# Pausing the weight steps in one-slot jobs and spacing the weights' sum from its use, in a Fourier transform with a mixture-of-experts layer

## The chip, the cores and the metric

The kernel runs on one core of a Trainium2 chip. The metric is device time in microseconds (us): the time from the start to the end of one execution on that core. Engines are named as in the profile: PE (TensorE, matmuls; PEld its weight loads), ACT (ScalarE), DVE (VectorE), POOL (GpSimd) and SP (SyncE, which here only issues DMAs).

## The reference

```python
X = np.fft.fft(x, axis=1)              # x: 8 x 1856 x 256
X = np.fft.fft(X, axis=2)
x = X.real.astype(np.float32).reshape(14848, 256)
...
g_idx = np.argmax(x @ w_group, axis=1)           # one of 4 groups for each token
e_idx = np.argmax(xg @ w_expert[g], axis=1)      # one of 4 experts of that group
h = np.maximum(xg[mask_e] @ w1[g, e], 0.0)       # 256 -> 1024
ye = h @ w2[g, e]                                # 1024 -> 256
out[tok_idx] = (g_w * e_w)[:, None] * ye         # two softmax weights
```

Each of 14848 tokens goes through the one expert (of 16) that its two argmaxes choose.

## The kernel before, in words

**Phase 1** computes the transform and the routing, and writes a row for each token to a DRAM table. **Phase 2** (`phase2`, L1335) runs the experts; the change lies there alone.

*Slots and jobs.* Tokens of one expert are gathered in slots of 128 rows. A job is one unit of weights and one to four slots. There are 44 jobs. Jobs 0 to 5 serve experts 0 to 2. Then each expert from 3 on has a four-slot job and a three-slot job, and all but the last are followed by a one-slot job for overflow rows, whose expert is known only at run time: job 8 (the ninth) is the first of these, then 11, 14 and so on to 41. So from job 6 on the work goes in groups of three jobs: four slots, three slots, one slot.

*One job.* Float32 values are split into a high and a low float16 half, and each product is made of three float16 matmuls (high x high, high x low, low x high). `layer1` (L1286) has eight groups; each makes one tile `ph` (128 x 512, 384 or 128 columns for four, three or one slots) with six matmuls, three for each half of the 256 inputs; the third and the sixth use the low half of the weights. ACT (L1299) and DVE (L1300) then take `ph` out into `hT`. `layer2` (L1305) makes one tile `py` for each slot with 24 matmuls of 256 columns; ACT takes it out into `y` (L1317) and POOL scatters the rows. PSUM has four banks for `ph` and two for `py`. The second layer of a job runs in the iteration of the next job, after that job's first layer: `pend` holds it.

*Weights.* The float32 weights of a unit (128 x 4096, 2 MB) land in `wst` by four DMAs of 512 KB that SP issues (`load_weights`, L1180). `split_steps` (L1193) is a generator that makes the float16 halves `whl` from them, one step for each call: four squares on ACT with a sum each (`junk`, `wacc`), two empty steps (`lag`), two small matmuls `pn` that sum over partitions (L1207) and one yield, then on DVE the scale (`e_ei`, two `e_v`, `winv`), and then four times a high half on ACT and a low half on DVE, 1024 columns at a time. Columns 0 to 2047 are the first layer's weights (parts 0 and 1), the rest the second layer's. The call after the last step takes the result and lets SP issue the loads of the next unit.

*Who hands out the steps.* `tick(g, t)` (L1457) is called after each group of a first layer with t = T1 x slots = 320 x slots, and after each slot of a second layer with t = T2 = 2570. It adds t to a balance and calls `weights()` (L1406) once for every 800 in it (`RATE2`). `weights()` runs one step of the first unit in `todo`, unless that unit's `whl` tile still belongs to a unit whose last job is not done: `free(todo[0]) > state["done"]`, where `done` becomes n - 1 at the end of iteration n (L1488). Then it returns False and the balance is set to 0. Units of long experts rotate over three `whl` tiles; the one-slot units have one of their own. `tick` also advances `g`, which casts (`xh`, L1258, L1260) and transposes (L1266, a DMA transpose from SP) the gathered rows of the next job.

```python
def tick(g, t):
    state["t"] += t
    rate = RATE if state["tail"] else RATE2
    while state["t"] >= rate:
        state["t"] = state["t"] - rate if weights() else 0
    tail()
    if not state["tail"]:
        next(g, None)
```

*The order on each engine.* The squares, halves and scales are issued through wrappers that keep them in program order (`self.V`, `self.A`); the rest of phase 2 is placed by the framework's scheduler, engine by engine. On each engine the order is fixed in the program, and each instruction waits for its operands there.

Of the kernel before, what the change touches and what calls it, by code (L numbers as in the profile page):

```python
# [46 lines left out]
LASTZ = 7  # L47
LATER = 3
OVER_AT = 4

RATE, RATE2, T1, T2 = 1000, 800, 320, 2570

# [199 lines left out]
def pow2s(V, pool, sumsq, n, tag, outs):  # L252

    ei = pool.tile([P, n], I32, name=f"{tag}_ei", tag=f"{tag}_ei")
    V.tensor_scalar(out=ei, in0=sumsq.bitcast(I32), scalar1=24, scalar2=None,
                    op0=ALU.logical_shift_right)
    vs = []
    for k, (m, a) in enumerate(outs):
        v = pool.tile([P, n], F32, name=f"{tag}_v{k}", tag=f"{tag}_v{k}")
        V.tensor_scalar(out=v.bitcast(I32), in0=ei, scalar1=m * E23, scalar2=a * E23,  # L260
                        op0=ALU.mult, op1=ALU.add)
        vs.append(v)
    return ei, vs


def top(ap):

    return ap.bitcast(mybir.dt.bfloat16).rearrange("p (n t) -> p n t", t=2)[:, :, 1]
# [34 lines left out]
class K:  # L303
# [886 lines left out]
                self.tc.keep_in_program_order(ins)  # L1190
        return st

    def split_steps(self, wp, st, V, A, M, pn, lag=0):  # L1193


        sm = self.sm
        acc = sm.tile([P, 2, 2], F32, name="wacc")
        junk = self.cp.tile([P, 4 * 257], mybir.dt.bfloat16, name="junk", tag="junk")
        for h in range(4):
            A.activation(junk[:, 0:1024], st[:, h * 1024:(h + 1) * 1024], AF.Square,  # L1200
                         accum_out=acc[:, h // 2, h % 2:h % 2 + 1])
            yield
        for _ in range(lag):
            yield
        acc = top(acc.rearrange("p a h -> p (a h)")).rearrange("p (a h) -> p a h", h=2)
        for h in range(2):
            M.matmul(pn, lhsT=self.one_b, rhs=acc[:, :, h], start=h == 0, stop=h == 1)  # L1207
        yield
        _, (sw, isw) = pow2s(V, sm, pn, 2, "e", [(-1, 198), (1, 56)])
        inv = sm.tile([P, 1], F32, name="winv", bufs=4)  # L1210
        V.tensor_tensor(out=inv, in0=isw[:, 0:1], in1=isw[:, 1:2], op=ALU.mult)
        yield
        w = wp.tile([P, 2, 4096], F16, name="whl")
        for i in range(4096 // WPART):
            s = slice(i * WPART, (i + 1) * WPART)
            h = i * WPART // 2048
            A.activation(w[:, 0, s], st[:, s], AF.Copy, scale=sw[:, h:h + 1])
            yield
            V.scalar_tensor_tensor(out=w[:, 1, s], in0=st[:, s], scalar=sw[:, h:h + 1],
                                   in1=w[:, 0, s], op0=ALU.mult, op1=ALU.subtract)  # L1220
            yield
        return w, inv
# [112 lines left out]
    def phase2(self, wp):  # L1335
        tc, nc = self.tc, self.nc
        wpa = self.wpa
        with tc.tile_pool(name="h", bufs=2, reuse_waits="tile") as hp, \
# [26 lines left out]
            def pools(u):  # L1365
                kind, e = units[u]
                if kind == "o":
                    return "wo", "wo"
                return "w", ("wa", "w2", "wx")[e % 3]
# [9 lines left out]
            st, ready, infos, xs, want = {}, {0: self.w0}, {}, {}, []  # L1379
            self.scratch = wpx.tile([P, 2, 4096], F16, name="whl").rearrange("p h n -> p (h n)")  # L1380
            state = dict(split=None, done=-1, t=0, tail=self.last_rows(), job=0)
            begun = lambda u: u < len(first) or state["job"] >= LATER

            def tail():
                if state["tail"]:
                    try:
                        next(state["tail"])
                    except StopIteration:
                        state["tail"] = None
                        pool["wo"] = later.enter_context(  # L1390
                            tc.tile_pool(name="wo", bufs=1, side="right", reuse_waits="tile"))
                    serve()
# [7 lines left out]
            def loads():  # L1400
                for u in todo:
                    if u not in st and all(pools(v)[0] != pools(u)[0] for v in st) and pools(u)[0] in pool \
                            and (units[u][0] == "s" or "o" in infos) and begun(u):
                        load(u)

            def weights():  # L1406

                if state["split"] is None:
                    if not todo or free(todo[0]) > state["done"] or (units[todo[0]][0] == "o" and "o" not in infos) \
                            or not begun(todo[0]):  # L1410
                        return False
                    loads()
                    pn = self.misc[:, 490 + 2 * todo[0]:492 + 2 * todo[0]] if state["tail"] else self.ps.tile([P, 2], F32, name="pn", tag="misc")
                    state["split"] = self.split_steps(pool[pools(todo[0])[1]], st[todo[0]],
                                                      self.V, self.A, nc.tensor, pn, 2)
                try:
                    next(state["split"])
                except StopIteration as e:
                    u = todo.pop(0)
                    ready[u], state["split"] = e.value, None  # L1420
                    del st[u]
                    loads()
                return True
# [25 lines left out]
            def prep(n):  # L1449
                if n < len(jobs):  # L1450
                    while n in want:
                        tail()
                    xs[n] = self.x0[n] if n < len(self.x0) else \
                        (yield from self.turn_steps(qp, *xs[n], *((self.V, self.A) if jobs[n][1] == "e" else
                                                                  (nc.vector, nc.scalar)), nc.sync))

            def tick(g, t):  # L1457
                state["t"] += t
                rate = RATE if state["tail"] else RATE2
                while state["t"] >= rate:  # L1460
# [4 lines that stand above are left out]
# [7 lines left out]
            for n, (u, kind, slots) in enumerate(jobs):  # L1472
                while u not in ready:
                    assert weights()
                w, inv = ready[u]
                state["job"] = n
                if n == OVER_AT:
                    infos["o"] = self.overflow_info(pool["wo"])
                g = prep(n + 1)
                xT, wt = xs.pop(n)  # L1480
                cw, toks = self.slot_weights(qp, wt, inv)
                fetch(n + 2)
                for _ in range(2 * len(jobs[2][2]) if n == 1 else 0):
                    next(g, None)
                hT = finish(self.layer1(hp, w, xT, len(slots)), lambda: tick(g, T1 * len(slots)))
                if pend:
                    finish(self.layer2(*pend), lambda: tick(g, T2))
                    state["done"] = n - 1  # L1488
                for _ in g:
                    pass  # L1490
                pend = (qp, w, hT, cw, toks)
# [79 lines left out]
```

## Time and profile before

| what | value |
|---|---|
| three runs | 891.83, 895.41, 895.62 us, median 895.41 |
| the profiled execution | 892.05 us, its span 890.2 us |
| PE busy in the span | 823.2 us (92%) |
| DVE, ACT, POOL busy | 546.6, 577.0, 313.5 us |
| first one-slot job that the change reaches | about 402 us into the span |

The page has one line for the busy time of each engine, then a line per engine with 40 slices of the span. The timeline merges instructions of the same kind that follow each other: start, length, engine, line, operation, out<-in, shape, count, and in brackets the idle time of the engine before them with what ended it. Times in it are from the span's start. Ends of matmuls are modelled.

### The profile page before, as it was taken

Reading aid. Unit: us, or ns where it says so; the run is one execution under the profiler, and the core shown is the slowest. Engines: PE = TensorE matmul, PEld = TensorE weight load, DVE = VectorE, ACT = ScalarE, POOL = GpSimd, SP = SyncE. Lnnn points to the kernel's source line nnn. Section 1 sums busy time; section 2 is a strip of 40 time slices with the busy share of each in tenths; the row PEclk is TensorE's granted clock in tenths of the full one; section 3 lists DMA queues with packets and bytes.
Section 4 is the critical chain, followed back from the end, with each engine's and each line's share of the span. In section 5 each row is a group of like instructions: output and inputs, shape, how many; then the busy total and the mean of one; then the engine's idle time right before and its main releaser. Section 6 shows DMA issues by size and latency. Waiting matters only on the chain.

```text
span 890.2 us, 17777 instructions
## 1 busy us (share of the span) xinstructions
PE 823.2 (92%) x6491; PEld 587.2 (66%) x6491; DVE 546.6 (61%) x1381; ACT 577.0 (65%) x1190; POOL 313.5 (35%) x326
## 2 busy tenths in 40 slices
PE   2799999889697999999999999999999999999996
PEld 0367666556455767776767676767676768686865
DVE  6479998579574656464747474747474756564440
ACT  2477676576633877586858585858686777775541
POOL 1032211412674524434343434344343435240303
PEclk9999999899999999999999999999999999999999
DMA  9677863364667355555646454646555746443201
GB/s 351 176 226 201 243 210 121 137 210 138 186 180 197 111 189 181 158 155 166 173 156 178 149 166 155 173 160 172 161 176 152 196 147 206 127 137 66 55 10 41
DMA packets 105515, 144.53 MB, mean 162 GB/s; under 512 B 75194, under 2 KB 77638, under 8 KB 103888
## 3 DMA queue, kind: packets, MB, share of 16 engines
q1 hardware_dynamic: 91360, 106.15, 39.4%
q0 software_dynamic: 13632, 36.99, 14.5%
q8 instruction: 52, 0.85, 0.4%
q10 hardware_dynamic: 432, 0.22, 0.1%
q14 instruction: 39, 0.32, 0.1%
HBM read 97.41 MB, written 31.72 MB: 145 GB/s over the span
## 4 chain that ended last, share of the span: by engine, by line
PE 58%; DVE 11%; issue 8%; ACT 5%; DMA 5%; POOL 2%; another core or an unknown queue 2%; SPq 1%; POOLq 0%; DVEq 0%; ACTq 0%
PE ph L1296 29%; PE py L1312 24%; DMA xT<-xh 3%; PE pu L281 2%; ACT whl L281 2%; POOL out L940 2%; PE pr L281 1%; DVE whl L281 1%; DMA wst<-w 1%; DVE xq L281 1%; ACT junk L281 1%; SPq L1266 1%; DVE ghl L281 1%; DVE xT L281 1%
## 5 line engine op out<-in xcount | busy, mean ns | idle before, releaser
L1312 PE MATMUL py<-whl,hT 128*128 128x256 f16 x2976 | 357.4, 273 | 13.6 <-ACT y L1317 9.8
L1296 PE MATMUL ph<-xT,whl 128*128 128x512 f16 (+2 forms) x2112 | 358.4, 318 | 10.6 <-DMA xT<-xh 4.8
L1312 PEld LDWEIGHTS <-hT 128*128 128x128 f16 x2976 | 289.2, 98 | 71.4 <-issue 15.2
L1300 DVE SCALAR_TENSOR_TENSOR hT<-ph,hT 128x512 f16<-128x512 f32 (+2 forms) x352 | 179.7, 529 | 194.1 <-ACT hT L1299 126.6
L1296 PEld LDWEIGHTS <-whl 128*128 128x128 f16 x2112 | 182.5, 98 | 134.1 <-issue 16.6
L940 POOL DMA_INDIRECT out<-y,tok x124 | 147.3, 1188 | 332.2 <-ACT y L1317 266.2
L1299 ACT ACTIVATE hT<-ph 128x512 f16<-128x512 f32 (+2 forms) x352 | 157.2, 473 | 116.0 <-PE ph L1296 68.1
L281 DVE SCALAR_TENSOR_TENSOR whl<-wst,e_v,whl 128x1024 f16<-128x1024 f32 x112 | 138.0, 1279 | 20.1 <-ACT whl L281 18.0
L1238 POOL DMA_INDIRECT xg<-XS,ii_s x100 | 105.5, 1055 | 86.7 <-ACT xh L1258 35.7
L281 ACT ACTIVATE whl<-wst,e_v 128x1024 f16<-128x1024 f32 x112 | 121.0, 1138 | 15.2 <-DVE e_v L281 11.4
L281 ACT ACTIVATE junk<-wst 128x1024 bf16<-128x1024 f32 x112 | 119.2, 1064 | 6.0 <-DMA wst<-w 5.1
L1317 ACT ACTIVATE y<-py,cws 128x256 f32<-128x256 f32 x124 | 57.2, 471 | 52.0 <-PE py L1312 41.2
L281 PE MATMUL pu<-CS,ghl 128*128 128x464 f16 (+3 forms) x384 | 83.8, 370 | 3.5 <-ACT ghl L281 3.5
L1260 DVE TENSOR_TENSOR xh<-xg,xh 128x256 f16<-128x256 f32 x112 | 46.3, 418 | 48.7 <-ACT xh L1258 35.7
L1258 ACT CAST xh<-xg 128x256 f16<-128x256 f32 x112 | 42.4, 402 | 38.6 <-DMA xT<-xh 34.7
L281 PEld LDWEIGHTS <-ghl 128*128 128x128 f16 (+1 forms) x384 | 44.5, 120 | 33.2 <-issue 3.6
L281 PEld LDWEIGHTS <-U 128*128 128x128 f16 x672 | 44.9, 100 | 19.2 <-issue 7.0
L281 PE MATMUL pr<-c,U 128*128 128x256 f16 x336 | 49.9, 286 | 4.9 <-DMA U<-un 2.5
L281 ACT CAST U<-pu 128x464 f16<-128x464 f32 (+3 forms) x64 | 32.8, 548 | 20.0 <-PE pu L281 19.0
L281 POOL DMA_DIRECT2D xq<-xq x12 | 11.0, 1072 | 88.5 <-ACT xT L281 27.1
L281 DVE TENSOR_TENSOR xq<-xq 128x514 f32<-128x514 f32 x40 | 25.4, 688 | 6.4 <-DMA xq<-xq 6.2
L281 ACT ACTIVATION_READ_ACCUMULATOR junk<-wst 128x1 f32 x112 | 23.2, 207 | 0.0
(184 smaller groups left out, 461.1 us busy)
## 6 DMA issues: line engine op xcount, KB each, us to landing
wst<-w SPq DMA_DIRECT2D x108, 512.0 KB
xq<-xq SPq DMA_DIRECT2D x8, 1028.0 KB
xq<-xq POOLq DMA_DIRECT2D x12, 514.0 KB
XS<-whl SPq DMA_DIRECT2D x6, 910.0 KB
CS<-cs SPq DMA_DIRECT2D x8, 464.5 KB
XS<-row SPq DMA_DIRECT2D x3, 1040.0 KB
XS<-row SPq DMA_DIRECT2D x3, 910.0 KB
XS<-xq SPq DMA_DIRECT2D x3, 910.0 KB
```

Source lines behind the costliest of these rows:

```text
L281: return self.tc.keep_in_program_order(f(*args, **kw))
L940: ins = self.nc.gpsimd.indirect_dma_start(out=out, out_offset=bass.IndirectOffsetOnAxis(ap=ap, axis=0), in_=in_, in_offset=None, bounds_ch ...
L1238: ins = self.nc.gpsimd.indirect_dma_start(out=xg[:, :].bitcast(I32), out_offset=None, in_=self.XS[:, :], in_offset=bass.IndirectOffsetOnAx ...
L1258: A.copy(xh[:, 0], xg[:, 0:D])
L1260: lo = V.tensor_tensor(out=xh[:, 1], in0=xg[:, 0:D], in1=xh[:, 0], op=ALU.subtract)
L1266: Q.dma_start(out=xT[:, :, j * P:(j + 1) * P], in_=xh, transpose=True)
L1296: nc.tensor.matmul(ph[:, 0:n * P], lhsT=w[:, wl, o:o + P], rhs=xT[:, xl * 2 + c, :], start=i == 0, stop=i == 5)
L1299: nc.scalar.activation(hT[:, f, 0], ph[:, 0:n * P], AF.Relu)
L1300: nc.vector.scalar_tensor_tensor(out=hT[:, f, 1], in0=ph[:, 0:n * P], scalar=0.0, in1=hT[:, f, 0], op0=ALU.max, op1=ALU.subtract)
L1312: nc.tensor.matmul(py, lhsT=hT[:, f, hl, j * P:(j + 1) * P], rhs=w[:, wl, 2048 + f * D:2048 + (f + 1) * D], start=i == 0, stop=i == 23)
L1317: nc.scalar.activation(y, py, AF.Copy, scale=cw)
```

## The change

From the ninth job on (`STEADY = 8`) `tick` hands out no step during the first layer of a job with one slot (there t is T1), and leaves the balance as it is; it still advances `g`. And for units whose split begins from the ninth job on, two more empty steps lie between the `pn` matmuls and the scale on DVE (`late` = 2).

```diff
+STEADY = 8
...
-    def split_steps(self, wp, st, V, A, M, pn, lag=0):
+    def split_steps(self, wp, st, V, A, M, pn, lag=0, late=0):
...
         for h in range(2):
             M.matmul(pn, lhsT=self.one_b, rhs=acc[:, :, h], start=h == 0, stop=h == 1)
-        yield
+        for _ in range(1 + late):
+            yield
         _, (sw, isw) = pow2s(V, sm, pn, 2, "e", [(-1, 198), (1, 56)])
...
                     state["split"] = self.split_steps(pool[pools(todo[0])[1]], st[todo[0]],
-                                                      self.V, self.A, nc.tensor, pn, 2)
+                                                      self.V, self.A, nc.tensor, pn, 2, 2 if state["job"] >= STEADY else 0)
...
             def tick(g, t):
+                if t == T1 and state["job"] >= STEADY:
+                    return next(g, None)
                 state["t"] += t
```

What that does to the order is seen at three places; the same repeats in each group of three jobs. Line numbers in the changed kernel are one or two higher.

ACT around a one-slot job's first layer, before: the last three evictions of the three-slot first layer, y of the second slot, the four high halves of the one-slot unit in a block, then casts and the y of the third and fourth slot.

```order
L1299 ACTIVATE hT<-ph 128x384
L281 ACTIVATE junk,wacc<-wst 128x1024
L1299 ACTIVATE hT<-ph 128x384 x3
L1317 ACTIVATE y<-py,cws 128x256
L281 ACTIVATE whl<-wst,e_v_5041 128x1024 x4
L1258 CAST xh<-xg 128x256
L1317 ACTIVATE y<-py,cws 128x256
L1258 CAST xh<-xg 128x256 x2
L1317 ACTIVATE y<-py,cws 128x256
L1299 ACTIVATE hT<-ph 128x128 x4
```

The same place now:

```order
L282 ACTIVATE junk,wacc<-wst 128x1024 x2
L1301 ACTIVATE hT<-ph 128x384
L1319 ACTIVATE y<-py,cws 128x256
L1301 ACTIVATE hT<-ph 128x384
L282 ACTIVATE whl<-wst,e_v_5101 128x1024 x2
L1319 ACTIVATE y<-py,cws 128x256
L282 ACTIVATE whl<-wst,e_v_5101 128x1024
L1260 CAST xh<-xg 128x256 x3
L1319 ACTIVATE y<-py,cws 128x256
L282 ACTIVATE whl<-wst,e_v_5101 128x1024
L1301 ACTIVATE hT<-ph 128x128 x4
```

The y of the third slot stands behind two high halves where it stood behind four, and the y of the fourth slot behind three high halves and three casts, with the fourth high half after it.

PE at the end of the first four groups of a one-slot first layer, before (`ph` and `py` with their numbers): the last matmul of each group, which reads the low half of part 1, stands directly ahead of the three-slot job's second layer.

```order
L1296 MATMUL ph_5207<-xT_4961,whl_5077 128x128
L1296 LDWEIGHTS whl_5077
L1296 MATMUL ph_5220<-xT_4961,whl_5077 128x128
L1296 LDWEIGHTS whl_5077
L1296 MATMUL ph_5232<-xT_4961,whl_5077 128x128
L1296 LDWEIGHTS whl_5077
L1296 MATMUL ph_5243<-xT_4961,whl_5077 128x128
L1296 LDWEIGHTS whl_5077
L1296 MATMUL ph_5243<-xT_4961,whl_5077 128x128
L1312 LDWEIGHTS hT_4945
L1312 MATMUL py_5301<-whl_4194,hT_4945 128x256
```

The same place now:

```order
L1314 LDWEIGHTS hT_4943
L1314 MATMUL py_5301<-whl_4194,hT_4943 128x256
L1298 LDWEIGHTS whl_5107
L1298 MATMUL ph_5207<-xT_4955,whl_5107 128x128
L1298 LDWEIGHTS whl_5107
L1298 MATMUL ph_5220<-xT_4955,whl_5107 128x128
L1298 LDWEIGHTS whl_5107
L1298 MATMUL ph_5232<-xT_4955,whl_5107 128x128
L1298 LDWEIGHTS whl_5107
L1298 MATMUL ph_5243<-xT_4955,whl_5107 128x128
```

Ahead of these four matmuls now stand 16 to 19 of the 24 matmuls of the first `py`. The second `pn` matmul moved too: 43 `py` matmuls stood between it and the one-slot first layer, and 31 stand there now.

DVE where a long unit's low halves end and the three-slot first layer begins, before: all four low halves are done ahead of that layer's first eviction.

```order
L281 SCALAR_TENSOR_TENSOR whl<-wst,e_v_4848,whl 128x1024
L1300 SCALAR_TENSOR_TENSOR hT<-ph,hT 128x512
L281 SCALAR_TENSOR_TENSOR whl<-wst,e_v_4848,whl 128x1024 x3
L281 TENSOR_SCALAR cws<-wt,winv 128x3
L281 CAST tok<-wt 128x3
L1260 TENSOR_TENSOR xh<-xg,xh 128x256
L1261 SCALAR_TENSOR_TENSOR wt<-ge_s,xg 128x2
L1300 SCALAR_TENSOR_TENSOR hT<-ph,hT 128x384
```

The same place now:

```order
L1302 SCALAR_TENSOR_TENSOR hT<-ph,hT 128x512
L282 SCALAR_TENSOR_TENSOR whl<-wst,e_v_4871,whl 128x1024 x3
L282 TENSOR_SCALAR cws<-wt,winv 128x3
L282 CAST tok<-wt 128x3
L1262 TENSOR_TENSOR xh<-xg,xh 128x256
L1263 SCALAR_TENSOR_TENSOR wt<-ge_s,xg 128x2
L1302 SCALAR_TENSOR_TENSOR hT<-ph,hT 128x384
L1262 TENSOR_TENSOR xh<-xg,xh 128x256
L1263 SCALAR_TENSOR_TENSOR wt<-ge_s,xg 128x2
L1302 SCALAR_TENSOR_TENSOR hT<-ph,hT 128x384
L282 SCALAR_TENSOR_TENSOR whl<-wst,e_v_4871,whl 128x1024
```

The fourth low half now stands behind two evictions of the three-slot first layer; SP's loads of the next long unit, which write the same `wst`, wait for it. SP's own order is the same in both.

## Rows read from the trace of the kernel before

**Rows 1.** The page: the span and the busy time of each engine.
```profile
span 890.2 us, 17777 instructions
...
PE 823.2 (92%) x6491; PEld 587.2 (66%) x6491; DVE 546.6 (61%) x1381; ACT 577.0 (65%) x1190; POOL 313.5 (35%) x326
```
**Rows 2.** Stretches of 40 us: length, PE, PEld, DVE, ACT, POOL busy; clock; DMA.
```profile
480.00:520.00 40.00, 38.68 (x313) 28.24 (x312) 23.32 (x54) 28.06 (x58) 15.01 (x14) 1.00 0.55 159
...
sum 400.00, PE 389.96 PEld 287.29 DVE 236.84 ACT 285.86 POOL 162.42; mean PE 39.00 PEld 28.73 DVE 23.68 ACT 28.59 POOL 16.24
```
**Rows 3.** Waits of PE, 395 to 800 us: us in total, times, longest.
```profile
PE py L1312 <- ACT y L1317: 7.4, 10, 0.8
PE ph L1296 <- DVE whl L281: 2.0, 7, 0.4
```
**Rows 4.** PE's timeline at the first and the last of nine one-slot jobs.
```profile
403.77 0.93 PE L1312 MATMUL py<-whl,hT 128*128 128x256 f16 x7 [0.81 <-ACT y L1317]
...
750.62 1.58 PE L1312 MATMUL py<-whl,hT 128*128 128x256 f16 x13 [0.81 <-ACT y L1317]
```
**Rows 5.** Timeline of all engines, 784 to 795 us: the tenth one-slot job.
```profile
787.18 0.15 DVE L281 TENSOR_SCALAR e_ei<-pn 128x2 int32<-128x2 int32 x1
...
791.18 1.50 PE L1296 MATMUL ph<-xT,whl 128*128 128x128 f16 x24
...
792.55 2.67 PE L1312 MATMUL py<-whl,hT 128*128 128x256 f16 x23
```
**Rows 6.** PE's timeline, 470 to 496 us: the one-slot job at 487.88.
```profile
473.47 1.14 PE L1296 MATMUL ph<-xT,whl 128*128 128x384 f16 x6
...
481.71 0.65 PE L1296 MATMUL ph<-xT,whl 128*128 128x384 f16 x3
...
482.85 0.17 PE L1207 MATMUL pn<-wacc,one_b 128*128 128x2 bf16 x1
...
485.26 2.78 PE L1312 MATMUL py<-whl,hT 128*128 128x256 f16 x24 [0.15 <-ACT y L1317]
487.88 1.22 PE L1296 MATMUL ph<-xT,whl 128*128 128x128 f16 x19
489.46 0.45 PE L1296 MATMUL ph<-xT,whl 128*128 128x128 f16 x5 [0.36 <-DVE whl L281]
490.73 5.07 PE L1312 MATMUL py<-whl,hT 128*128 128x256 f16 x45 [0.81 <-ACT y L1317]
```
**Rows 7.** ACT's timeline in the same place.
```profile
484.36 0.49 ACT L1299 ACTIVATE hT<-ph 128x384 f16<-128x384 f32 x1 [2.23 <-PE pn L1207]
...
485.74 4.27 ACT L281 ACTIVATE whl<-wst,e_v 128x1024 f16<-128x1024 f32 x4 [0.53 <-DVE e_ei L281]
489.91 0.39 ACT L1258 CAST xh<-xg 128x256 f16<-128x256 f32 x1
490.21 0.47 ACT L1317 ACTIVATE y<-py,cws 128x256 f32<-128x256 f32 x1
490.58 0.70 ACT L1258 CAST xh<-xg 128x256 f16<-128x256 f32 x2
```
**Rows 8.** DVE's timeline in the same place.
```profile
485.36 0.15 DVE L281 TENSOR_SCALAR e_ei<-pn 128x2 int32<-128x2 int32 x1
...
486.92 4.87 DVE L281 SCALAR_TENSOR_TENSOR whl<-wst,e_v,whl 128x1024 f16<-128x1024 f32 x4 [0.95 <-ACT whl L281]
```
**Rows 9.** SP's timeline: DMA issues, and one stretch without weight loads.
```profile
475.64 2.68 SPq L1188 DMA_DIRECT2D wst<-w  x4
484.35 3.81 SPq L1266 DMA_TRANSPOSE xT<-xh  x3
...
773.24 16.58 SPq L1266 DMA_TRANSPOSE xT<-xh  x6
```
**Rows 10.** Waits of all engines, 380 to 760 us.
```profile
ACT xh L1258 <- DMA xT<-xh: 16.6, 9, 2.5
...
ACT hT L1299 <- PE pn L1207: 12.6, 8, 2.4
```

## The prediction

> **What bounds it now.** I read the page first: TensorE is busy 823.2 of 890.2 us, no other engine more than 65% [rows 1]. Then the table of stretches, because the change begins at the ninth job: from 360 to 760 us TensorE works 389.96 of 400 us, and the granted clock is 1.00 throughout, its upper level of 2.4 GHz [rows 2]. So TensorE is the bound here, there is nothing to win from the clock, and all that an order of steps can give back is about 10 us of shown idle time. The list of waits names who ends it: ACT's y 7.4 us in ten waits, DVE's whl 2.0 us in seven [rows 3]. TensorE's timeline says where: each time a one-slot job's first layer runs. It issues 19 of the 24 narrow matmuls, waits for whl, issues 5, then waits 0.81 us for y before the second layer goes on; first until 403.77, last until 750.62, nine times [rows 4], one every 43.4 us.
>
> A shown gap is too small, since a matmul's end overlaps the next start: 24 narrow matmuls take 1.50 us [rows 5] and 19 take 1.22 [rows 6], so one follows the other by 0.28/5 = 0.056 us while each is drawn 0.21 long. The true loss is the gap + 0.16. In the same way 24 wide ones (py) in 2.78 and 45 in 5.07 give 0.11 us for each py [rows 6].
>
> Loss now: 9 x (0.81 + 0.16) = 8.7; whl 2.0 + 7 x 0.16 = 3.1; the one 0.15 gap at 485.26 [rows 6] 0.3. Together **12.1 us**, 1.34 for each of nine jobs.
>
> Why the wait is there, in the job at 487.88 (call this T0). ACT runs four whl conversions in one block, 485.74 to 490.01; the eviction of the third slot's y stands behind them and a cast and ends at 490.21 + 0.47 = 490.68, and TensorE goes on at 490.73 [rows 6, 7]. There are two py banks, so the next py group needs that one. DVE's second low half ends near 486.92 + 2 x 1.22 = 489.36, and the last five narrow matmuls start at 489.46 [rows 6, 8]. Both hang on e_ei, the first instruction after the weights' sum, at 485.36 or T0 - 2.5, though the sum's second matmul ran at 482.85 [rows 6, 8]. In between ACT stood 2.23 us: it began the eviction at 484.36 although the matmuls before it are drawn as ended at 482.36 [rows 6, 7]; DVE takes e_ei only behind that eviction.
>
> **The change, part by part.** *No steps in the one-slot first layer: 0 us.* When a one-slot job runs, the job before it is not marked done (that is set after its second layer, at the end of this very job), the next unit's tile belongs to it, and weights() returns at once. The guard skips a question that was answered no, and the order of all engines shows no step removed there. If I am wrong on that, a step not handed out costs later what ACT spends on it, 1.07 us [rows 7], beside TensorE.
>
> *Two more empty steps after the sum.* A long unit now takes 19 calls and not 17, so it ends in the third call of the three-slot job, the one-slot unit starts two calls later and is itself two longer: its squares and sum move by two calls, e_ei and the eight halves by four. The three-slot job hands out (8 x 960 + 4 x 2570)/800 = 22 calls; 3 + 19 = 22 fit, so nothing is forced out in a lump. No instruction is added. What moves is order:
> - TensorE: the sum's second matmul stands 31 py before T0 (43 before), at T0 - 3.4. The last matmul of each of the first four narrow groups (the one that needs the second low half) now comes 16 to 19 py later.
> - ACT: two conversions, the third slot's y, one conversion, three casts, the fourth slot's y, one conversion. Before: four, cast, y, two casts, y.
> - DVE and SP: the long unit's last low half moves behind the second three-slot eviction, and the four weight loads that SP issues after it (475.64 now [rows 9]) go with it, by 1 to 2 us (estimate: one to two three-slot groups of 6 matmuls, 1.14 us each [rows 6]).
>
> When is e_ei now? Without any lag at T0 - 3.4 + 0.2; DVE takes it behind the eviction of the last three-slot group, and two whole squares stand ahead of that on ACT, so I put the early end at T0 - 2.6. The late end adds to T0 - 3.2 a lag as that of [rows 7], up to 2.2: T0 - 1.0. I take **T0 - 2.1**, half that lag, near the mean of the nine (12.6 us over nine jobs is 1.4, [rows 10]). From e_ei on, by [rows 7, 8]: first conversion after 0.38, each 1.07; the low half starts 1.18 after its high half, each 1.22; y 0.47; three casts 1.09. So first low half T0 + 0.7, third slot's y T0 + 0.9, second low half T0 + 1.9, fourth slot's y T0 + 3.5.
>
> TensorE asks for them at: first low half after 8 narrow matmuls, T0 + 0.45: **0.2 us lost**. Third slot's y after 20, T0 + 1.1 (+ 0.2): in time. Second low half after 16 py more, T0 + 2.9: in time by 1 us. Fourth slot's y, with the second py group, T0 + 4.0: in time by 0.5, unless the casts wait for their buffers, which DMA transposes behind the later weight loads must empty first. I give that another **0.2**. A tenth one-slot job, at 791.18, loses nothing now [rows 5] and gets the new order too. So 10 x 0.4 = 4.0 us stay.
>
> Sum: 892.05 (the profiled execution) - 12.1 + 4.0 = 883.95. The three timed runs lie at 891.83, 895.41 and 895.62 with median 895.41; with the profiled one their mean is 893.7, 1.7 above the one I sum against. I forecast 883.95 + 1.7 = **885.6 us**. Ends of this case: nothing lost, 880 + 0; 0.9 lost per job, 889 + 1.7.
>
> A run of this kernel repeats within about 0.4%, so 0.5% is what I call a difference.
>
> **Rivals.**
> *A, the wait changes its name.* If TensorE's release of the sum lags by the full 2.2 us, e_ei is at T0 - 1.0, the first low half at T0 + 1.8, and TensorE waits 1.35 us after 8 matmuls: 10 x 1.35 = 13.5, 892.05 - 12.1 + 13.5 + 1.7 = 895.2. For it: eight waits of this kind, the longest 2.4 us [rows 10], each while a weight load is under way [rows 9], and the sum is now nearer to T0. Against: the mean is 1.4, and at 791.18, with no weight load among SP's issues from 773 to 790 [rows 9], e_ei came at T0 - 4.0 and nothing was lost [rows 5]. The Trainium skill (Perfetto Trace Analysis, Tensor Engine Instruction) says a matmul's shown end is an estimate and that others are released only when PSUM has acknowledged the writes. By the drawn ends e_ei is at T0 - 2.6 and the kernel at 881 + 1.7, by late releases it is rival A; the 2.0 us between 482.36 and 484.36 say that the drawn end is not the release here.
>
> *B, slower: the casts block the fourth slot's y.* The three casts now stand ahead of it on ACT, each needs an xh buffer that a transpose empties, and the transposes stand on SP's queue behind the four loads, 475.64 and 484.35 [rows 9]. Now the first cast runs unhindered at 489.91, T0 + 2.0 [rows 7]. If the last transpose ends at T0 + 5, y is done at T0 + 5 + 0.36 + 0.47 and TensorE loses 1.9 us a job: 892.05 - 12.1 + 19 + 1.7 = 900.6. It turns slower than before when that end is later than T0 + 4.5. For it: casts of this line already waited 16.6 us for transposes in nine places [rows 10]. Against: a slack of two us, and a shift of the loads by 1 to 2.
>
> *C, the gap stays whatever the order, since two py banks are too few*: 893.7. At 791.18 the same two banks lose nothing [rows 5]. The Trainium skill (Perfetto Trace Analysis, Optimization Strategy) says that a gap that repeats can mean too few buffers; by that this change gains nothing. The row at 791.18 speaks against it.
>
> **How the numbers follow.** The forecast's case 0.64, A 0.22, B 0.10, C 0.04. Faster by over 0.5% (below 889.2 against 893.7) is the forecast's case less its worst end: 0.62. The same: that end, A and C: 0.28. Slower: B, 0.10. The range runs from 879 (nothing lost, and a run like the lowest one shown) to 896 (above A and C); it leaves B out.
>
> **What would show it.** Right: TensorE's gaps before py after a one-slot first layer gone, and 5 matmuls at the end of it no longer waiting; ACT's y between the second and third conversion; narrow matmuls waiting for whl at most 0.3 us after the eighth. A would show as one wait for whl over 1 us in each one-slot job; B as py waiting for y after 24 py, with ACT's xh waiting for DMA just before; a wrong first term as squares or conversions missing between one-slot and four-slot job. If TensorE's gaps go and the time stays, my sum's premise that TensorE sets the end is wrong.

## The result, and the profile after

| what | before | after |
|---|---|---|
| median of five runs | 895.41 us (891.83 to 896.77) | 885.35 us (884.32 to 886.72) |
| profiled execution, its span | 892.05, 890.2 us | 884.32, 882.5 us |
| PE busy from 360 to 760 us | 389.96 us | 394.73 us |

The ratio is 0.9898, with a 95% interval of 0.9872 to 0.9923. Forecast was 885.6 us.

The page of the changed kernel, against [rows 1]: TensorE does the same work in a shorter span.

```profile
span 882.5 us, 17744 instructions
...
PE 821.8 (93%) x6491; PEld 586.6 (66%) x6491; DVE 550.4 (62%) x1381; ACT 578.8 (66%) x1190; POOL 324.7 (37%) x326
```

The waits of PE, 395 to 800 us, against [rows 3] (columns as there):

```profile
PE ph L1298 <- DVE whl L282: 4.5, 8, 0.7
PE ph L1298 <- ACT whl L282: 0.4, 2, 0.2
PE pn L1208 <- ACT junk L282: 0.2, 1, 0.2
```

The ten gaps before py are gone. The waits for whl have grown from 2.0 to 4.5 us, and they stand elsewhere. PE's timeline of the changed kernel, against [rows 4, 6]: the end of job 8, then the jobs whose first layers start (T0) at 398.65, 440.55 and, without its first wait, 483.83.

```profile
361.80 1.50 PE L1298 MATMUL ph<-xT,whl 128*128 128x128 f16 x24
...
395.24 0.17 PE L1208 MATMUL pn<-wacc,one_b 128*128 128x2 bf16 x1
...
398.65 1.28 PE L1298 MATMUL ph<-xT,whl 128*128 128x128 f16 x20
...
437.36 0.17 PE L1208 MATMUL pn<-wacc,one_b 128*128 128x2 bf16 x1
...
440.55 0.61 PE L1298 MATMUL ph<-xT,whl 128*128 128x128 f16 x8
441.59 0.84 PE L1298 MATMUL ph<-xT,whl 128*128 128x128 f16 x12 [0.43 <-DVE whl L282]
442.27 2.24 PE L1314 MATMUL py<-whl,hT 128*128 128x256 f16 x19
...
484.07 0.62 PE L1298 MATMUL ph<-xT,whl 128*128 128x128 f16 x8 [0.24 <-ACT whl L282]
485.39 0.84 PE L1298 MATMUL ph<-xT,whl 128*128 128x128 f16 x12 [0.70 <-DVE whl L282]
```

In the first of the nine jobs nothing is waited for; in the other eight TensorE stops after eight narrow matmuls for the first low half, 0.4 to 0.7 us shown. ACT's and DVE's timelines of the changed kernel, against [rows 7, 8], tell why:

```profile
439.06 2.19 ACT L282 ACTIVATE whl<-wst,e_v 128x1024 f16<-128x1024 f32 x2 [2.38 <-DVE e_v L282]
441.16 0.45 ACT L1319 ACTIVATE y<-py,cws 128x256 f32<-128x256 f32 x1
...
443.72 0.41 ACT L1260 CAST xh<-xg 128x256 f16<-128x256 f32 x1 [0.46 <-DMA xT<-xh]
444.03 0.47 ACT L1319 ACTIVATE y<-py,cws 128x256 f32<-128x256 f32 x1
```

```profile
395.52 0.15 DVE L282 TENSOR_SCALAR e_ei<-pn 128x2 int32<-128x2 int32 x1
...
438.67 0.16 DVE L282 TENSOR_SCALAR e_ei<-pn 128x2 int32<-128x2 int32 x1 [1.39 <-PE py L1314]
...
440.25 3.73 DVE L282 SCALAR_TENSOR_TENSOR whl<-wst,e_v,whl 128x1024 f16<-128x1024 f32 x3 [0.95 <-ACT whl L282]
...
482.47 0.16 DVE L282 TENSOR_SCALAR e_ei<-pn 128x2 int32<-128x2 int32 x1 [2.08 <-PE py L1314]
```

At 395.52 e_ei follows the second pn (395.24) at once, 3.1 us ahead of T0. At 438.67 it comes 1.31 us after pn started (437.36), at T0 - 1.9, with DVE idle for 1.39 us ahead of it, and at 482.47 at T0 - 1.4. Over the steady part that is one row of the waits of all engines, 380 to 760 us, against [rows 10]:

```profile
DVE e_ei L282 <- PE py L1314: 13.1, 8, 2.1
...
ACT xh L1260 <- DMA xT<-xh: 11.5, 12, 2.3
```

**Where the 7.7 us between the two profiled executions lie.** The second half of job 8 begins at 364.14 us before and at 361.80 now: 2.3 us are there ahead of the first place where the two orders differ. From there to the same place in the last of the nine jobs (755.53 and 749.18) it takes 391.39 and 387.38 us, 4.0 less, and 1.4 more are gained in the last jobs: 39.02 us from 797.46 to 836.48 before and 37.59 from 791.08 to 828.67 now, with 166 and 153 py between these marks, since 13 of them now run earlier. So the change is worth 5.4 us in this pair, and the 2.3 lie where the orders are still the same.

### The profile page after: what moved, and what is told of

It is laid out like the page before. It is cut to its first block, busy times and chain, and to the rows that moved or that the text cites. A ratio compares the mean times of both kernels' runs of the same rounds, so it can differ in the third digit from the quotient of the medians.

```text
span 882.5 us, 17744 instructions
## 1 busy us (share of the span) xinstructions
PE 821.8 (93%) x6491; PEld 586.6 (66%) x6491; DVE 550.4 (62%) x1381; ACT 578.8 (66%) x1190; POOL 324.7 (37%) x326
## 4 chain that ended last, share of the span: by engine, by line
PE 59%; DVE 11%; issue 8%; ACT 5%; DMA 4%; another core or an unknown queue 2%; POOL 2%; SPq 0%; POOLq 0%; DVEq 0%; ACTq 0%
PE ph L1298 28%; PE py L1314 26%; DVE whl L282 3%; DMA xT<-xh 2%; PE pr L282 2%; ACT junk L282 2%; PE pu L282 2%; ACT whl L282 2%; POOL out L941 2%; DMA wst<-w 1%; DVE xq L282 1%; DVE ghl L282 1%; DVE xT L282 1%; ACT hT L1301 1%
## 5 line engine op out<-in xcount | busy, mean ns | idle before, releaser
L1240 POOL DMA_INDIRECT xg<-XS,ii_s x100 | 116.6, 1166 | 116.9 <-ACT hT L1301 64.9
L282 DVE SCALAR_TENSOR_TENSOR whl<-wst,e_v,whl 128x1024 f16<-128x1024 f32 x112 | 140.1, 1279 | 20.3 <-ACT whl L282 16.8
L282 ACT ACTIVATE whl<-wst,e_v 128x1024 f16<-128x1024 f32 x112 | 123.9, 1140 | 26.9 <-DVE e_v L282 24.6
L282 DVE SCALAR_TENSOR_TENSOR ghl<-BD,x_v,ghl 128x512 f16<-128x512 f32 (+1 forms) x30 | 21.8, 780 | 2.1 <-ACT ghl L282 2.1
```

The costliest lines, as they stand in the source:

```text
L282: return self.tc.keep_in_program_order(f(*args, **kw))
L1240: ins = self.nc.gpsimd.indirect_dma_start(out=xg[:, :].bitcast(I32), out_offset=None, in_=self.XS[:, :], in_offset=bass.IndirectOffsetOnAx ...
```

## The experiments

All twelve ran where the kernel before takes 865 us, not 895. They ran on four chips, and its median lay between 864.88 and 865.59 us on each; which chip the first comparison ran on is not on record, so another chip and another condition of the same one are both possible. Each run was timed against the kernel before on its own chip. Times are medians, brackets are 95% intervals of the ratio, and every kernel keeps the guard (the two lines in `tick`).

**The guard alone.** `late` is left out. (The other half needs no run: `late` without the guard has, row by row, the order of the whole change on all five engines.)

```diff
...
-    self.V, self.A, nc.tensor, pn, 2, 2 if state["job"] >= STEADY else 0)
+    self.V, self.A, nc.tensor, pn, 2, 0)
...
```

> Only the first part of the change: no steps are handed out in a one-slot job's first layer from the ninth job on; the two empty steps are left out. Row by row the order of all five engines is the one of the kernel before. My theory (the guard skips a question that is always answered no): the time of the kernel before, ratio 1.00 within 0.2%, with the same nine gaps of TensorE before py, some 0.8 us each. Rival (the guard does part of the work of the change): 3 to 5 us less than before. The run also says how far two executions of one order differ: the changed kernel's profiled execution was 2.3 us ahead at 362 us, where the change has not begun, and I expect a difference of that size here too.

Measured: 864.50 us, ratio 1.0001 [0.9985, 1.0018]. The guard does nothing, as forecast. But the nine gaps that I expected with it aren't there. PE's waits of this kernel, 370 to 770 us:

```profile
PE py L1314 <- ACT y L1319: 0.4, 2, 0.2
PE ph L1298 <- DVE hT L1302: 0.4, 1, 0.4
```

The same place as [rows 6], in PE's timeline, then ACT's and DVE's (T0 is 467.69):

```profile
462.98 0.17 PE L1208 MATMUL pn<-wacc,one_b 128*128 128x2 bf16 x1
463.00 4.85 PE L1314 MATMUL py<-whl,hT 128*128 128x256 f16 x43
467.69 1.50 PE L1298 MATMUL ph<-xT,whl 128*128 128x128 f16 x24
469.17 5.07 PE L1314 MATMUL py<-whl,hT 128*128 128x256 f16 x45
```

```profile
464.19 4.27 ACT L282 ACTIVATE whl<-wst,e_v 128x1024 f16<-128x1024 f32 x4 [0.74 <-DVE e_v L282]
468.36 0.39 ACT L1260 CAST xh<-xg 128x256 f16<-128x256 f32 x1
468.66 0.47 ACT L1319 ACTIVATE y<-py,cws 128x256 f32<-128x256 f32 x1
```

```profile
463.76 0.15 DVE L282 TENSOR_SCALAR e_ei<-pn 128x2 int32<-128x2 int32 x1
```

The same instructions in the same order, and e_ei stands at T0 - 3.9 and not at T0 - 2.5. ACT never waits for pn here, where it waited 12.6 us in eight places [rows 10]. So y is done at T0 + 1.44 and py goes on at T0 + 1.48. By the spacing of 0.056 us, py could go on at T0 + 1.34 after 24 narrow matmuls, and over the nine jobs y is done between T0 + 1.14 and T0 + 1.67: this order has a margin of about nothing even here. From the second half of job 8 to that of the last of the nine jobs this kernel takes 380.2 us (346.15 to 726.31), 11.2 less than the same order in the first pair; the loss that I had read from the gaps was 12.1.

What differs is when TensorE's releases arrive, the semaphore updates on which the other engines wait. I set each update of the trace against the last matmul that sends one and is drawn as ended before it, which gives the smallest lag that the trace allows. From 360 to 800 us, in the kernel before, 73 of 353 updates came over 0.3 us behind that end, up to 2.0; in the changed kernel 54 of 333, up to 1.5; here none of 386 over 0.05, and none in the other eleven runs. ACT's and DVE's updates were on time everywhere, as far as they are recorded: in the first pair records are missing (in the kernel before, 353 updates for 376 matmuls that send one, and on ACT 483 for 573), while here they are complete on both (386 and 581). Whether the recording itself has a part in the lateness, no run tells.

**Each half of `late` alone.** Only the long units' splits, or only the one-slot units', get the two steps:

```diff
+    2 if state["job"] >= STEADY and units[todo[0]][0] == "s" else 0)
...
+    2 if state["job"] >= STEADY and units[todo[0]][0] == "o" else 0)
```

> The two empty steps only in the long units' splits; the one-slot unit starts two calls later for that, but its scale follows its sum after one call, as before. TensorE's order is that of the changed kernel (20 narrow matmuls, 19 py, 4 narrow), while on ACT the third slot's y stands behind three conversions and not two. Theory Y (what cost the time is where y stands on ACT): y comes one conversion, 1.07 us, later than in the changed kernel, TensorE waits for it 0.3 to 0.8 us in nine jobs, 3 to 7 us slower than the changed kernel, about 890. Rival N (what helped is TensorE's own new order, with part of the narrow matmuls behind py): as the changed kernel, 885, without gaps before py.

> The two empty steps only in the one-slot units' splits. TensorE's order around the one-slot first layer is that of the kernel before (43 py behind the sum, 24 narrow matmuls in a block, 45 py), while on ACT the third slot's y stands behind three conversions and a cast and not behind four and a cast. Theory Y: y is done 1.07 us earlier, the nine gaps of 0.97 us before py shrink to 0.2 or less, the waits of the last five narrow matmuls for whl stay (3 us together); 7 to 9 us less than before, 886 to 889. Rival N: the gaps stay, 893 to 896.

Measured: 864.66 us, 0.9998 [0.9983, 1.0012], and 866.14 us, 1.0017 [0.9990, 1.0044]. Neither theory is tested: with no late release there is nothing to win by either.

**The weight load held back.** After a long unit's split, the next load waits for a copy on DVE beside the one-slot unit's scale (`hold` counts ten calls down to it):

```diff
+    if state["hold"] and state["split"]:
+        state["hold"] -= 1
+        if not state["hold"]:
+            self.V.tensor_copy(out=self.sm.tile([P, 1], F32, name="held"), in_=state["old"][:, 4095:4096])
+            loads()
...
```

> The changed kernel with the long unit's weight load held back: its four DMAs wait for a one-column copy on DVE that stands beside the one-slot unit's scale, some 8 us later than before, so that no weight load is in flight when the one-slot unit's sum runs. The order on ACT changes with it (a cast before the first conversion; y behind three conversions for the third slot). Theory L (the release of the sum by TensorE arrives 1.1 to 1.8 us after the drawn end of pn because a weight load is in flight): e_ei follows the second pn within 0.5 us, the narrow matmuls' waits for whl (4.5 us shown in the changed kernel) go, 4 to 6 us less than the changed kernel, 880. Rival D (the delay belongs to TensorE's own order, load or not): e_ei still 1.1 to 1.8 us behind pn, the same waits, 885 or slower.

Measured: 867.35 us, 1.0020 [1.0000, 1.0039]. It says nothing on theory L, since no release was late here without it either. What makes them late stays open.

**The whole change again.**

> The whole change once more. On the chip of the first four runs the kernel before took 865 us, its trace showed no release of TensorE later than 0.1 us behind the drawn end of the matmul, e_ei stood at T0 - 3.9 and only three of the gaps before py were left, 0.7 us together. Theory R (the loss that the change wins back comes from releases by TensorE that arrive 1 to 2 us late; where they come in time there is nothing to win): on a chip without late releases, ratio to the kernel before 0.998 to 1.004; on one with them, 0.985 to 0.993 as in the first comparison. Rival O (the order is better by itself): a ratio of 0.99 on either.

Measured: 865.89 us, 0.9995 [0.9972, 1.0018]: theory R. The order is not better by itself. PE's timeline, then ACT's and DVE's, with T0 at 472.90:

```profile
469.71 0.17 PE L1208 MATMUL pn<-wacc,one_b 128*128 128x2 bf16 x1
...
472.90 1.28 PE L1298 MATMUL ph<-xT,whl 128*128 128x128 f16 x20
```

```profile
470.34 2.19 ACT L282 ACTIVATE whl<-wst,e_v 128x1024 f16<-128x1024 f32 x2 [1.30 <-DVE e_v L282]
472.44 0.46 ACT L1319 ACTIVATE y<-py,cws 128x256 f32<-128x256 f32 x1
```

```profile
469.94 0.16 DVE L282 TENSOR_SCALAR e_ei<-pn 128x2 int32<-128x2 int32 x1 [0.31 <-PE pn L1208]
...
471.52 3.72 DVE L282 SCALAR_TENSOR_TENSOR whl<-wst,e_v,whl 128x1024 f16<-128x1024 f32 x3 [0.71 <-ACT whl L282]
```

Here e_ei follows pn by 0.23 us, at T0 - 3.0. The third slot's y is done at T0 + 0.0 (needed at T0 + 1.1), the first low half at 471.52 + 1.24, T0 - 0.14 (needed at T0 + 0.45). So the order has a margin of 0.6 us (0.3 in two of the nine jobs, where the first conversion starts later), where the kernel before has about none. That is the new theory, M, and it can be tested here by making the conversions late.

The same run shows rival B, past its slack, in two of the nine jobs. PE's waits, 370 to 770 us, then PE's and ACT's timeline at the longer one, T0 at 556.70:

```profile
PE py L1314 <- ACT y L1319: 1.5, 2, 1.2
```

```profile
562.06 3.11 PE L1314 MATMUL py<-whl,hT 128*128 128x256 f16 x27 [1.24 <-ACT y L1319]
```

```profile
558.74 0.41 ACT L1260 CAST xh<-xg 128x256 f16<-128x256 f32 x1 [1.01 <-DMA xT<-xh]
560.85 0.78 ACT L1260 CAST xh<-xg 128x256 f16<-128x256 f32 x2 [1.70 <-DMA xT<-xh]
561.54 0.47 ACT L1319 ACTIVATE y<-py,cws 128x256 f32<-128x256 f32 x1
```

The three casts wait for transposes, and the fourth slot's y behind them is done at T0 + 5.3, where TensorE could use it at T0 + 4.0. The two gaps cost 1.5 + 2 x 0.16 = 1.8 us. Gaps of this kind stand in the two runs of the long units' half as well (0.5 us in the first; 0.8 and 1.0 in the second).

**A conversion more, ahead of the four high halves** of each one-slot unit from the ninth job on (`pad` = 1), its result thrown away, without the two empty steps; then half a one (512 columns), and a whole one with the long units' part of the change.

```diff
+        for _ in range(pad):
+            A.activation(junk[:, 0:1024], st[:, 0:1024], AF.Copy, scale=sw[:, 0:1])
         for i in range(4096 // WPART):
...
```

> The kernel before (with the guard, which moves nothing) with a fifth conversion on ACT directly ahead of the four high halves of each one-slot unit from the ninth job on, its result thrown away: 1.07 us more between e_ei and y, as a late release would make it. Where releases come in time, y of the third slot is done at T0 + 1.4 without it and at T0 + 2.5 with it, while TensorE needs it at T0 + 1.5. Theory Y: a gap of about 0.9 us before py in each of nine jobs comes back, and a wait of up to 0.2 for whl before the last five narrow matmuls: 8 to 11 us slower than the kernel before, 1.010 to 1.013. Rival (TensorE has slack there, the gap needs more than late conversions): within 3 us of the kernel before.

Measured: 877.16 us, 1.0131 [1.0087, 1.0175], 11.8 us more. The gaps are back, nine of them, where [rows 4, 6] have them. PE's waits, 370 to 770 us:

```profile
PE py L1316 <- ACT y L1321: 7.6, 9, 0.9
```

PE's and ACT's timeline at one:

```profile
471.23 1.72 PE L1300 MATMUL ph<-xT,whl 128*128 128x128 f16 x24
473.82 5.18 PE L1316 MATMUL py<-whl,hT 128*128 128x256 f16 x46 [0.87 <-ACT y L1321]
```

```profile
467.79 1.15 ACT L282 ACTIVATE junk<-wst,e_v 128x1024 bf16<-128x1024 f32 x1 [0.81 <-DVE e_v L282]
468.85 4.25 ACT L282 ACTIVATE whl<-wst,e_v 128x1024 f16<-128x1024 f32 x4
473.01 0.39 ACT L1262 CAST xh<-xg 128x256 f16<-128x256 f32 x1
473.30 0.46 ACT L1321 ACTIVATE y<-py,cws 128x256 f32<-128x256 f32 x1
```

One conversion of 1.07 us brings back the gaps before py of the first pair: late conversions are enough for them, and y's place on ACT is how they reach TensorE. The wait for whl that I expected shows only as a longer block, 1.72 us for 24 narrow matmuls where it takes 1.50 [rows 5].

> The kernel before with an extra conversion of 512 columns, not 1024, ahead of the four high halves of each one-slot unit from the ninth job on: some 0.6 us. Theory M on a chip without late releases: 0.6 less the margin of 0.06 in each of nine or ten jobs, 4.5 to 6 us slower than the kernel before, half of what the whole conversion cost (11.8 us): ratio 1.005 to 1.007. Rival T (there is a threshold, the extra work is either hidden or costs all of a period): 0 or some 12 us. On a chip with late releases the same 0.6 us in each job comes on top.

Measured: 869.80 us, 1.0068 [1.0042, 1.0094], 4.9 us by the medians and 5.9 by the ratio. No threshold: half the delay costs about half. PE's waits, 370 to 770 us:

```profile
PE py L1316 <- ACT y L1321: 4.4, 10, 0.7
```

> The two empty steps in the long units' splits alone, and a fifth conversion of 1024 columns (1.07 us) ahead of the four high halves, as in the run of the kernel before with one. Theory M without late releases: first low half at T0 + 0.94, needed at T0 + 0.45, 0.5 us lost; third slot's y then at T0 + 2.1, needed at T0 + 1.6, 0.5 lost; 1.0 in each of nine or ten jobs, 8 to 10 us slower than the kernel before, ratio 1.009 to 1.012. Rival N (20 narrow matmuls, 19 py and 4 narrow give TensorE other work while it waits): under 5 us.

Measured: 874.16 us, 1.0106 [1.0085, 1.0127], with both waits that theory M named:

```profile
PE ph L1300 <- DVE whl L282: 3.9, 9, 0.5
PE py L1316 <- ACT y L1321: 2.4, 9, 0.3
```

TensorE's new order (20, 19 py, 4) is there, and 9.3 us of the time are lost all the same, against 11.8 with the old order in the other comparison. Rival N, which had under 5, falls.

**The whole change with half a conversion more, and with a whole one.** The same lines, and the fourth square shortened to 512 columns so that ACT's order stays that of the change; the sum that sets the unit's scale then leaves out the other 512.

```diff
-            A.activation(junk[:, 0:1024], st[:, h * 1024:(h + 1) * 1024], AF.Square,
+            k = 512 if pad and h == 3 else 1024
+            A.activation(junk[:, 0:k], st[:, h * 1024:h * 1024 + k], AF.Square,
```

> The whole change with an extra conversion of 512 columns (0.6 us) ahead of the four high halves of each one-slot unit, as in the run of the kernel before that lost 5.9 us by it. So that ACT's order around the one-slot layer stays that of the change (two conversions, the third slot's y, one, three casts, the fourth slot's y, one), the unit's fourth square takes 512 of its 1024 columns; the sum that sets the unit's scale then leaves out the other 512. Theory M on a chip without late releases: the margin of 0.6 us takes the whole delay, within 1.5 us of the kernel before, ratio 0.998 to 1.002. Rival (the change has no more margin than the kernel before): 5 to 6 us slower, 1.006.

Measured: 867.96 us, 1.0015 [0.9990, 1.0039]. The half conversion that cost the kernel before 0.68% costs the change 0.15%, an interval that holds zero. Of PE's waits, 370 to 770 us, the one that the delay would bring is left in two places only, 0.2 us in one of the nine jobs and 0.7 in the tenth one-slot job (beside it stands one of 2.2 us for an eviction in a four-slot job, as others of 0.2 to 1.5 us do in these runs):

```profile
PE ph L1301 <- DVE whl L282: 0.9, 2, 0.7
```

> The same with an extra conversion of 1024 columns (1.07 us), the fourth square again of 512. Theory M without late releases: 1.07 less 0.6 is 0.5 us in each of nine or ten jobs, as a wait of narrow matmuls for the first low half after the eighth, none for y: 3 to 6 us slower than the kernel before, ratio 1.004 to 1.007, against 11.8 us for the kernel before with that conversion and 9.2 for the long units' part alone. Rival: 9 to 12 us, 1.011 to 1.014.

Measured: 870.78 us, 1.0058 [1.0036, 1.0081], 5.2 us by the medians against 11.8, and the wait is the one that the changed kernel showed in the first pair:

```profile
PE ph L1301 <- DVE whl L282: 3.8, 8, 0.6
```

**The halves once more**, in the hope of late releases:

> The two empty steps in the one-slot units' splits alone, once more. Theory M (each order has a margin, the time by which y and the low halves come before TensorE needs them when releases are in time; a late release costs what exceeds the margin, in each of nine jobs). Margins from the traces without late releases: kernel before 0.06 us (y at T0 + 1.44, needed at T0 + 1.5), the whole change 0.6 (first low half at T0 - 0.14, needed at T0 + 0.45), this one 0.9 (second low half at T0 + 0.13, needed at T0 + 1.06). If this chip shows releases late by 1.4 us: 0.5 us lost in each job against 1.4 in the kernel before, ratio 0.990 to 0.992. If it shows none: 0.998 to 1.004 as before. Rival N (TensorE's new order is what helps): ratio 1.00 on either.

> The two empty steps in the long units' splits alone, once more. Its margins: first low half 0.6 us, third slot's y 0.1 (done at T0 + 1.03, needed at T0 + 1.1). Theory M: with releases late by 1.1 to 1.6 us it loses 1.0 to 1.5 us in each job, as the kernel before, ratio 0.998 to 1.004; without late releases the same ratio. Rival N: with late releases as the whole change, ratio 0.99.

Measured: 867.98 us, 1.0032 [1.0013, 1.0051], and 863.60 us, 0.9990 [0.9972, 1.0008], with no late releases. That the one-slot half would do better than the whole change where releases are late is worked out from its margin of 0.9 us and was not seen. Where they are in time it costs 0.3% in this comparison, though its trace shows no wait that would explain it: TensorE waits 0.2 us in all from 370 to 770 us.

No version was faster than both kernels: where nothing is late the kernel before has no gaps to take away, and where releases are late no experiment ran.

## Why the prediction was right, and where not

The number was right, 885.6 for 885.35; the sum behind it was right in its first half and too good in its second.

- **Loss now, 12.1 us: right**, and now measured on its own. The same order without late releases is 11.2 us shorter over the nine jobs, and 1.3 of its time there are still waits by the same rule.
- **The guard, 0 us: right**, 1.0001.
- **e_ei at T0 - 2.1, the step that failed.** It came at T0 - 1.9 to T0 - 1.4 in eight of nine jobs, within the range given and toward its late end, and at T0 - 3.1 in one. Part of it is the order: 31 py stand behind the sum in the first of the nine jobs alone and 29 in the other eight, so the sum stands at T0 - 3.2 there and not at T0 - 3.4. The rest is the lag: 1.1 to 1.6 us in these eight jobs, counted from T0 - 3.0, where e_ei stands when nothing is late, and I had taken 1.1. I had taken a mean lag; the first low half is the first thing that a lag above the margin hits, so a job that is 0.5 us late isn't paid back by one that is early.
- **First low half, 0.2 us lost a job: mis-sized.** The eight waits of 4.5 us are, with 0.16 each, 5.8, that is 0.64 a job over nine; the waits for the high half (0.4, two) and for pn (0.2, one) add 1.1 in the same way. 6.9 us stay in the nine jobs, where I had 3.6. The sign that I had named for the forecast's case, at most 0.3 us after the eighth narrow matmul, was not met (0.4 to 0.7 shown), and neither was rival A's, over 1 us.
- **Third slot's y in time: right.** At 441.16 + 0.45 = 441.61, T0 + 1.06 against 0.9 forecast, and no wait for it; where e_ei is at T0 - 1.4 it is done at T0 + 1.6, past T0 + 1.1, and TensorE, held up by the first low half, does not notice.
- **Fourth slot's y, 0.2 lost for casts blocked by transposes: not seen.** At 443.72 a cast does wait 0.46 us for a transpose, and y is done at 444.50, T0 + 3.95; TensorE, itself late by the first wait, shows no gap. Rival B was there in kind and stayed within its slack in this execution; in the other condition it went past it and cost 1.8 us in two jobs.
- **The tenth job, 0.4: nothing**, as before.

By the same rule 12.1 less 6.9 is 5.2 us won, and the marks in the trace give 5.4, where the sum had 8.1. The rule closes: the nine jobs less TensorE's waits take 391.39 - 12.1 = 379.3 us before and 380.16 - 1.3 = 378.9 in the run of the guard. In the changed order, which has 11 py of 0.11 us more in this stretch, they take 387.38 - 6.9 = 380.5, and 383.74 - 3.1 = 380.6 where the whole change ran again (349.52 to 733.26, with the 1.5 us above, 1.0 in two waits for evictions, and 4 x 0.16). So the waits counted here are the difference. That the number met the median to 0.3 us is luck: the profiled execution of the changed kernel was also 2.3 us ahead at 362 us, where the two orders do not differ yet. In the twelve later runs that same mark, with the same order ahead of it, lay between 346.15 and 351.19 us, so a pair of executions can differ by that much. The forecast's case was the likeliest one and did come, with a good part of rival A in it: A had the wait at 1.35 us a job, and it is 0.64.

**Rival C** (the gap stays whatever the order, since two py banks are too few) falls: in the run of the guard the same two banks run through nine jobs with 0.4 us of waits for y. The Trainium skill says that a gap that repeats can mean too few buffers (Perfetto Trace Analysis, Optimization Strategy). Here the same two banks had the gap or not, as y was late or not; whether a third bank would have hidden a late y was not tried. **Rival A's ground** holds better than I weighed it. The Trainium skill (Perfetto Trace Analysis, Tensor Engine Instruction) says that a matmul's shown end is an estimate and that the release comes with PSUM's acknowledgement: in the first pair up to 2.0 us at the least lay between the two, in the other runs 0.05 at most, so the drawn end can be right or far off for the same instruction.

What is shown: that late conversions cause the gap, that each order has a margin beyond which a delay is paid (about 0 before, about 0.6 with the change), that the waits counted here make up the difference in the nine jobs, and that without late releases the change is worth nothing. What is only argued: that the late releases are what made the conversions late in all of these jobs, since no run could set them, and which half of the change carries the gain there. What makes the releases late is open.

## What to carry to other kernels

A gap on the bounding engine can be made by an instruction that is late, not by its place; compute for each consumer when its operand is there and when it is needed, and read the margin, since a reorder is worth only the delay that exceeds the old margin and fits in the new one. Before a reorder is judged by one comparison, look whether the delay that it covers is in every run: this one gave 1% in one and nothing in another. Where the lateness can't be had on demand, an added operation of known length in front of the consumer measures the margin well.

## What the runs showed of the hardware that was not expected

TensorE's releases were up to 2.0 us late, at the least, in the two profiles of the first comparison and never more than 0.05 us in twelve others, with the same instructions and, in the run of the guard, the same order. Late ones come in clumps: in the changed kernel the releases of two py and a pn with drawn ends from 437.52 to 438.09 all arrive between 438.61 and 438.71, so they were held back and not slowed. In that stretch a weight load is just ending. SP's timeline of the changed kernel:

```profile
388.18 1.79 SPq L1189 DMA_DIRECT2D wst<-w  x4
...
430.05 1.76 SPq L1189 DMA_DIRECT2D wst<-w  x4
```

With the load at 388.18 a clump ended at 393.88, ahead of the second pn (395.24), and that is the one job in which e_ei was in time; with the load at 430.05 it ended at 438.71, behind it. From 360 to 800 us, all 54 late updates of the changed kernel and 72 of the 73 of the kernel before came between 4.0 us behind the issue of a weight load and 1.1 us behind the end of its last packet, and 19 of the 20 loads of that stretch have some. So in the first pair the lateness goes with the loads; but loads are in flight in the other runs too, and nothing is late in those, so a load alone does not do it. The order of the kernel before took 29.4 us less in the run of the guard (spans 860.8 and 890.2); 11.2 of them lie in the nine jobs, 18.0 ahead of 364 us, whose cause is open, and 0.2 after 756.
